# Moving two weight-conversion steps on VectorE, and renumbering PSUM banks, in a fused attention and feed-forward kernel

## The chip, the core and the metric

The kernel runs on one core of a Trainium2 chip. The metric is device time in microseconds (us) of one execution. TensorE is called PE here, with PEld for its weight loads; VectorE is DVE, ScalarE is ACT, GpSimd is POOL, and SP is the engine whose queue issues most DMAs.

## What is computed

Routing attention over 4 batches, 8 heads, 768 positions and 64 dimensions, followed by a feed-forward layer of width 2048 on the 3072 tokens:

```python
q_assign = np.argmax(np.einsum('bhsd,hcd->bhsc', q_n, c_n), axis=-1)   # 16 clusters a head
k_assign = np.argmax(np.einsum('bhsd,hcd->bhsc', k_n, c_n), axis=-1)
mask = q_assign[:, :, :, None] == k_assign[:, :, None, :]
scores = np.where(mask, scale * np.matmul(q, k.transpose(0, 1, 3, 2)), -1e9)
attn = softmax(scores)                       # less the row maximum, over sum + 1e-9
x = matmul(attn, v)                          # laid out as (B*S, H*D) = (3072, 512)
h = x @ w_in                                 # (3072, 2048)
g = h * erf(softplus(h))
out = g @ w_out                              # (3072, 512)
```

## The kernel before

**Two stages.** Attention comes first. It works on 16 pairs: one batch and two heads each, the two heads one below the other on the 128 partitions. Behind it comes the feed-forward layer in 6 chunks of 512 tokens, computed with fast matrix multiplication schemes, so that many sums of blocks stand beside fewer products. In attention, and in most of the feed-forward part, every engine's instructions run in the order in which the code issues them (`InOrder`, whose inner call is the line L132 that nearly all instructions of the profile carry). Each engine is therefore a queue: an instruction that waits holds all behind it on the same engine.

**A pair's six sixths.** `period(p, i)` (L1361) issues sixth i of pair p. A sixth handles two units; a unit u is 128 keys against 384 queries (one half of the queries), for both heads. Sixths 0 to 2 are the first half of the queries, 3 to 5 the second. In a sixth PE's order is, with the helper of each step:

- at sixths 0 and 3 `turn`, which brings row shifts into place;
- `step_ahead` (L1347), a step of `maxima_step` (L460) for later units: four bf16 matmuls into the one tile `wide`, then DVE's reduction `nmx<-wide` over it, the row maxima. A second such step follows in the same sixth, and its first matmuls need the first reduction to be over, for there is only one `wide`;
- `products` (L513): scores into the tile `sc`, two buffers in turn; `scores` (L526) adds the mask;
- at sixth 3 `similarities` (L391) for the pair after next, into the bank `turned[1]`;
- `curve`: ACT's exponentials from `sc` into `pr`;
- `attend`: matmuls of the sixth before, with `v`, into `turned[0]` (first half) or `turned[1]` (second half);
- at the ends of sixths 0 and 3 the first part of `divide` (L574) for the half just finished: matmuls `turned<-more_out,minus`, which sum over the keys what POOL has added up, into the *other* `turned` bank. At sixth 3 that is `turned[1]`, which held the similarities. ACT then takes logarithm and exponential of it, and DVE the quotient (`den`, two `turned<-turned,inv`, and `more_out<-den,turned`) in the sixth that follows.

On POOL `accumulate` (L549) adds the `pr` tiles of a half, unit by unit: five additions a half, each on the result of the one before. `divide`'s matmuls need the last of them.

**The choice of clusters.** `choose` (L404) is a generator that `period` moves on a step at a time through `routing[0]`. Its steps on DVE: a transposition `sims<-turned` of the similarities, a maximum over 16 clusters (`sc<-sims`, into a score bank), the comparison `hot<-sims,sc`, and two more transpositions in sixths 5 and 0. Sixth 3 issues the first three.

**The weights' conversion.** While attention runs, the feed-forward weights are fetched in steps n (256 KB of 64-bit words each) and converted for 22 of 32 steps, two steps a pair, in pairs 1 to 11: n1 = 2p − 1 and n2 = 2p (`early` tells whether a step exists). A step passes through

- `size` and `rest` on ACT (L305, L308), writing into the weight tile `w` and into the fetched place;
- `bounded` (L316) on DVE: a maximum with 2.0 on `w`, 128x512 fp32;
- `sign` (L320) on ACT, which reads and writes the fetched place, not `w`;
- `shifted` (L327) on DVE: a shift left by 3 on `w` as uint32, after `bounded`;
- `summed` (L331) on POOL: adds the fetched place to `w`, after `shifted`, and then issues the fetch of a later step (five further on) into the same place, on SP.

Step n1 has its `bounded`, `sign` and `shifted` in sixth 3 and its `summed` in sixth 4, ahead of that sixth's additions of `accumulate`. The other step, n2, has `bounded` and `shifted` in sixth 0 of the next pair and `summed` in sixth 1.

**Banks in the feed-forward part.** `whole_bank` (L699) counts `n_banks` up and takes entry `n_banks % 8` of a list: entries 0 to 5 are fresh tiles of a pool with six buffers (`bank` in the profile), entries 6 and 7 are the fixed tiles `turned[0]` and `turned[1]`. Chunks 2 to 5 run `hidden49` (L1039) and then `project26` (L1234). `hidden49` computes seven outer products `o`; each begins (L1088) by taking four banks X, N, Y and Z in this order. X is written by four products in turn (`m1`, `m6`, `m7`, `m4`), with an eviction after each; N by `m5`, the second product of the first outer one. `project26` takes 26 banks for as many products and evicts each one product later, the last ones after its loop. A chunk takes 28 + 26 = 54 banks, so its start in the list of eight moves on by 6 from chunk to chunk.

Of the kernel before, what the change touches and what calls it, by code (L numbers as in the profile page):

```python
# [140 lines left out]
def kernel(  # L141
# [174 lines left out]
    def bounded(n):  # L316
        w = w_steps[n][0]
        ve.tensor_scalar(out=w, in0=w, scalar1=2.0, scalar2=None, op0=ALU.max)
# [8 lines left out]
    def shifted(n):  # L327
        w = w_steps[n][0].bitcast(U32)
        ve.tensor_scalar(out=w, in0=w, scalar1=3, scalar2=None, op0=ALU.logical_shift_left)
# [61 lines left out]
    def similarities(p):  # L391

        if p >= NPAIR:
            return
        st = pairs[p]
        st["psim"] = turned[1][:, 0:HW]
        for g in range(4):
            te.matmul(
                st["psim"][2 * C * g : 2 * C * (g + 1)], lhsT=ccT[:, p % HP],
                rhs=st["qk"[g // 2] + "T"][:, (g % 2) * HW : (g % 2 + 1) * HW],  # L400
                start=True, stop=True,
            )
# [57 lines left out]
    def maxima_step(p, i, sm=wide, behind=False, cut=HW):  # L460

        st = pairs[p]
        nmx = maxima[p % 2]
        t, half = divmod(i, 2)
        keys = slice(cut, S) if half else slice(0, cut)
        width = keys.stop - keys.start

        def passes(a, b, start, rows):
            for e in range(2):
                r = slice(e * D + rows.start, e * D + rows.stop)  # L470
                te.matmul(
                    sm[:, e, 0:width], lhsT=st[a][r, t * P : (t + 1) * P],
                    rhs=st[b][r, keys], start=start, stop=not start,
                )

        passes("qv", "kv", True, slice(0, D))
        if behind:
            yield
        passes("qm", "km", False, slice(Q, D) if behind else slice(0, D))
        if behind:  # L480
            yield
        ve.tensor_reduce(
            out=nmx[:, :, t, half], in_=sm[:, :, 0:width], axis=AX.X, op=ALU.max, negate=True
        )
        if i in (NJ - 1, 2 * NJ - 1):
            h = i // NJ
            ve.tensor_reduce(
                out=lowest[h][:, :, ::D].rearrange("p t e -> p e t"),
                in_=nmx[:, :, h * HJ : (h + 1) * HJ], axis=AX.X, op=ALU.min,
            )  # L490
            turns.append((p, h))
# [204 lines left out]
    n_banks = [0]  # L696
# [342 lines left out]
    def hidden49(n):  # L1039
# [33 lines left out]
        def second_forms(which):  # L1073
            for get, new in ((all_own, xb_own), (all_more, lambda i: xb[:, i, 4:])):
                b11, b21, b22, b12 = (get(o) for o in (1, 2, 3, 7))
                for out, a, b in {
                    0: [(new(0), b12, b11), (new(1), b22, new(0)), (b12, b22, b12)],
                    1: [(new(1), b21, new(1))],
                }[which]:
                    minus_of(out, a, b, ge)  # L1080
# [7 lines left out]
        def begin(k):  # L1088
            o = OUTER[k]
            state[o] = {nm: whole_bank() for nm in "XNYZ"}  # L1090
            state[o].update({nm.lower(): t.rearrange("p (j t) -> p j t", t=P) for nm, t in state[o].items()})
            state[o]["m5"] = temps[k % 3]
# [107 lines left out]
        def second_gate():  # L1200
# [5 lines left out]
            (5, m5): lambda: gates_of[2:], (5, m2): lambda: first_steps,  # L1206
            (5, m6): second_gate, (6, m1): lambda: later["soft"][1:], (6, m6): lambda: later["erf"],
        }
        for k, o in enumerate(OUTER):
            begin(k)  # L1210
            p = OUTER[k - 1]
            if k == 0:
                steps = [(m1, o), (m5, o), (m2, o), (m6, o)]
            elif k == 1:
                steps = [(m1, o), (m5, o), (m7, p), (m3, p), (m6, o), (m4, p), (m2, o)]
            elif k < 6:
                steps = [(m1, o), (m7, p), (m5, o), (m3, p), (m4, p), (m6, o), (m2, o)]
            else:
                steps = [(m1, o), (m7, p), (m5, o), (m3, p), (m6, o), (m4, p), (m2, o), (m7, o), (m3, o), (m4, o)]
            for i, (f, which) in enumerate(steps):  # L1220
                f(which)
                for work in extra_of.get((k, f), lambda: [])() if which == o else ():
                    work()
                if k in (0, 4) and f == m2:
                    second_forms(k // 4)
# [115 lines left out]
    def run(work):  # L1341
        for _ in work:
            pass
# [3 lines left out]
    def step_ahead(u, behind=False):  # L1347
        p, i = divmod(u + NJ, 2 * NJ)
        cut = NARROW if u >= 2 * NJ and u // 2 % HJ < HJ - 1 else HW
        steps = maxima_step(p, i, behind=behind, cut=cut) if p < NPAIR else iter(())  # L1350
        if not behind:
            run(steps)
        return steps
# [4 lines left out]
    routing = [iter(())]  # L1358
    part = [iter(())]

    def period(p, i):  # L1361
        u = 2 * NJ * p + 2 * i
        n1, n2 = 2 * p - 1, 2 * p
        early = lambda n: 0 <= n < N_EARLY

        def mask(place):
            which = (MASKS if p else FIRST_MASKS).get((i, place))
            if which:
                return masks(p + 1, *which, turned[0 if i in (0, 5) else 1], place > 1)
            return lambda: None  # L1370

        if u > 0:
            for which in turns if i in (0, 3) else ():
                turn(*which)
                turns.remove(which)
            step_ahead(u)
        mask(0)()
        next(part[0], None)
        if i == 5:
            next(routing[0], None)  # L1380
        if i == 0 and p:
            run(routing[0])
        if u == 2:
            next(routing[0])
        products(u)
        products(u + 1)
        mask(1)()
        second = step_ahead(u + 1, True) if u > 0 else iter(())
        next(second, None)
        rows = D if u == 0 or u + NJ >= len(units) else Q  # L1390
        scores(u, rows)
        next(second, None)
        if i:
            next(second, None)
        next(part[0], None)
        scores(u + 1, rows)
        later = mask(2)
        if i == 0:
            next(second, None)
        if i == 3:  # L1400
            similarities(p + 2)
            routing[0] = choose(p + 2, sc_of[u + 1][:, 0], True)
        if i == 0:
            later()
            later = lambda: None
        curve(u)
        later()
        curve(u + 1)
        if u == 0:
            step_ahead(1)  # L1410
            similarities(1)
            routing[0] = choose(1, turned[0])
            next(routing[0])
            next(routing[0])
            vectors(1, "q")
            vectors(1, "k")
        if i == 0 and early(n1 - 1):
            bounded(n1 - 1)
            shifted(n1 - 1)
        elif i == 1 and early(n1):  # L1420
            size_and_rest(n1)
        elif i == 3 and early(n1):
            bounded(n1)
            sign(n1)
        elif i == 5 and early(n2):
            rest(n2)
        for _ in range(min(len(forms), FORMS.get(p, {}).get(i, 0))):
            forms.pop(0)[0]()
        if i == 3:
            for _ in range(3):  # L1430
                next(routing[0], None)
            if early(n1):
                shifted(n1)
        elif i == 1:
            load(p + 1, "v", v, vp)
            if p == 0:
                run(routing[0])
                transposes(2, "q")
        elif i == 2:
            transposes(p + 2, "k")  # L1440
        elif i == 4:
            vectors(p + 2, "k")
            vectors(p + 2, "q")
        elif i == 5:
            transposes(p + 3, "q")
        if u > 0:
            if i == 4 and early(n1):
                summed(n1)
            for w in (u - 2, u - 1):
                accumulate(w)  # L1450
            if i == 1 and early(n1 - 1):
                summed(n1 - 1)
            if i % HJ == 1 and p in POOL_FORMS and forms:
                forms.pop(0)[1]()
            for w in (u - 2, u - 1):
                attend(w)
            if i % HJ == 0:
                part[0] = divide(u - 1)
                next(part[0])
        if i == 0 and early(n1 - 1):  # L1460
            sign(n1 - 1)
        if i == 3 and early(n2):
            size(n2)
# [186 lines left out]
```

## Time and profile before

| | us |
|---|---|
| median of 3 runs (964.34 to 964.9) | 964.86 |
| profiled execution, time | 965.18 |
| profiled execution, span from first to last instruction | 963.5 |
| attention's last `minus` matmuls, from the start of the span | 414.96 |
| from chunk 4's first product (780.83) to chunk 5's (870.19) | 89.36 |

The granted PE clock is 1.00 over the span. A timeline line has the start in us from the beginning of the span, the length in us, the engine, line and operation, what it writes `<-` what it reads, the shape and the count; brackets give idle time of the engine before it and what ended that. Neighbouring instructions of one kind are merged into a line, with their count. A matmul's end is modelled; its start is measured. Several instructions that work on `w` share the form `w_in<-w_in`: of these, fp32 is `bounded` and uint32 is `shifted`.

### The profile page before, as it was taken

Reading aid. Unit: us, or ns where it says so; the run is one execution under the profiler, and the core shown is the slowest. Engines: PE = TensorE matmul, PEld = TensorE weight load, DVE = VectorE, ACT = ScalarE, POOL = GpSimd, SP = SyncE. Lnnn points to the kernel's source line nnn. Section 1 sums busy time; section 2 is a strip of 40 time slices with the busy share of each in tenths; the row PEclk is TensorE's granted clock in tenths of the full one; section 3 lists DMA queues with packets and bytes.
Section 4 is the critical chain, followed back from the end, with each engine's and each line's share of the span. In section 5 each row is a group of like instructions: output and inputs, shape, how many; then the busy total and the mean of one; then the engine's idle time right before and its main releaser. Section 6 shows DMA issues by size and latency. Waiting matters only on the chain.

```text
span 963.5 us, 22508 instructions
## 1 busy us (share of the span) xinstructions
PE 953.1 (99%) x8954; PEld 721.8 (75%) x8954; DVE 765.4 (79%) x1322; ACT 561.2 (58%) x853; POOL 543.6 (56%) x385
## 2 busy tenths in 40 slices
PE   8999999999999999999999999999999999999998
PEld 3555555555555555588888888998999899989987
DVE  8888888888888886878879878488847966795787
ACT  3778888888887666557624442564258226714651
POOL 1678877777777888935789902550353054206500
PEclk9999999999999999999999999999999999999999
DMA  9444444446444311272994349653564438254523
GB/s 220 79 109 111 110 108 107 109 109 176 89 111 107 71 35 35 65 277 66 183 206 192 147 163 236 207 187 116 191 199 130 162 135 262 77 185 152 157 88 110
DMA packets 180920, 134.41 MB, mean 140 GB/s; under 512 B 131888, under 2 KB 141616, under 8 KB 180784
## 3 DMA queue, kind: packets, MB, share of 16 engines
q1 hardware_dynamic: 173600, 123.37, 44.1%
q0 software_dynamic: 4720, 9.18, 5.4%
q8 instruction: 71, 1.16, 0.5%
q10 hardware_dynamic: 2496, 0.43, 0.2%
q14 instruction: 33, 0.27, 0.1%
HBM read 99.39 MB, written 35.39 MB: 140 GB/s over the span
## 4 chain that ended last, share of the span: by engine, by line
PE 94%; DMA 2%; DVE 2%; POOL 1%; issue 1%; ACT 0%; SPq 0%; DVEq 0%; ACTq 0%; POOLq 0%
PE bank L132 41%; PE turned L132 31%; PE sc L132 16%; PE wide L132 6%; POOL more_out L132 1%; DVE nmx L132 1%; DMA more_in<-a_dram 1%; DMA g_more<-in_moe_w_out_dram 0%; DMA in_k<-in_k_dram 0%; DMA in_q<-in_q_dram 0%; SPq L132 0%; DVE kT L132 0%; ACT pr L132 0%; DVE turned L132 0%; DVE sims L132 0%
## 5 line engine op out<-in xcount | busy, mean ns | idle before, releaser
L132 DVE TENSOR_REDUCE nmx<-wide 128x2 f32<-128x512 f32 (+2 forms) x189 | 180.6, 955 | 62.3 <-PE wide L132 59.7
L132 POOL TENSOR_TENSOR more_out<-more_out,pr 128x768 f32<-128x768 f32 x128 | 217.2, 1697 | 17.4 <-ACT pr L132 9.8
L132 ACT ACTIVATE pr<-sc 128x768 f32<-128x768 f32 x192 | 148.6, 810 | 73.1 <-PE wide L132 54.6
L132 PE MATMUL turned<-pr,in_v 128*32 128x193 f32 x3072 | 144.8, 330 | 0.0
L132 PEld LDWEIGHTS turned<-pr,in_v 128*32 128x32 f32 x3072 | 91.5, 109 | 51.5 <-issue 22.0
L132 DVE TENSOR_TENSOR g<-g,bank 128x512 f32<-128x512 f32 (+1 forms) x139 | 77.9, 578 | 50.7 <-PE bank L132 45.8
L132 PE MATMUL bank<-x_own,w_in 128*128 128x128 f32 (+1 forms) x712 | 106.6, 296 | 0.0
L132 POOL TENSOR_TENSOR x_own<-x_own 128x512 f32<-128x512 f32 x16 | 23.0, 1449 | 146.5 <-DVE x_own L132 133.7
L132 PE MATMUL sc<-qT,kT 64*128 64x384 f32 x528 | 98.5, 486 | 0.0
L132 PEld LDWEIGHTS bank<-x_own,w_in 128*128 128x128 f32 x712 | 94.2, 192 | 4.7 <-DVE g L132 0.8
L132 DVE TENSOR_TENSOR g<-g 128x512 f32<-128x512 f32 x114 | 78.9, 692 | 19.8 <-PE bank L132 14.0
L132 POOL TENSOR_TENSOR more_out<-pr,pr 128x768 f32<-128x768 f32 x32 | 58.9, 1840 | 40.4 <-ACT pr L132 40.4
L132 POOL TENSOR_TENSOR g<-g,osb 128x512 f32<-128x512 f32 x40 | 51.9, 1312 | 49.4 <-DVE g L132 35.7
L132 PE MATMUL bank<-w_out,g 128*128 128x256 f32 x336 | 77.0, 379 | 0.0
L132 PEld LDWEIGHTS bank<-w_out,g 128*128 128x128 f32 x336 | 63.7, 190 | 9.0 <-DVE g L132 0.3
L132 PE MATMUL bank<-g_more,g 128*128 128x256 f32 x288 | 68.3, 380 | 0.0
L132 PE MATMUL wide<-kv,qv 64*128 64x256 bf16 (+2 forms) x378 | 64.0, 328 | 1.1 <-ACT km L132 0.6
L132 PE MATMUL wide<-km,qm 64*128 64x256 bf16 (+3 forms) x378 | 62.5, 327 | 0.0
L132 PEld LDWEIGHTS sc<-qT,kT 64*128 64x128 f32 x528 | 47.9, 187 | 19.2 <-ACT inv L132 2.9
L132 DVE TENSOR_TENSOR g<-a_s,g 128x512 f32<-128x512 f32 x64 | 59.7, 969 | 3.1 <-ACT a_s L132 3.1
L132 ACT ACT_TABLE_LOAD x40 | 51.3, 1283 | 18.5 <-DVE g L132 17.8
L132 PEld LDWEIGHTS bank<-g_more,g 128*128 128x128 f32 x288 | 54.5, 190 | 8.1 <-issue 0.8
(214 smaller groups left out, 1961.3 us busy)
## 6 DMA issues: line engine op xcount, KB each, us to landing
g_more<-b_dram SPq DMA_DIRECT2D x48, 512.0 KB, 3.3
w_in<-a_dram SPq DMA_DIRECT2D x64, 256.0 KB, 3.6
more_in<-a_dram SPq DMA_DIRECT2D x48, 256.0 KB, 3.4
x_own<-in_moe_w_in_dram SPq DMA_DIRECT2D x13, 512.0 KB, 4.0
in_v<-in_v_dram SPq DMA_DIRECT2D x32, 192.0 KB, 3.0
x_dram<-more_out SPq DMA_DIRECT2D x128, 48.0 KB, 2.2
x_own<-x_dram SPq DMA_DIRECT2D x6, 1024.0 KB, 5.5
in_k<-in_k_dram SPq DMA_DIRECT2D x59, 96.0 KB, 2.6
```

The lines of the kernel that those rows point to most:

```text
L132: ins = getattr(self.engine, name)(*args, **kw)
```

## The change

It moves two DVE instructions of step n1 and changes the count of banks. `bounded(n1)` goes from ahead of `choose`'s transposition to right behind it, still in sixth 3. `shifted(n1)` goes from the end of sixth 3 into sixth 4, behind that sixth's first `step_ahead` and so behind its first reduction of row maxima. The order on DVE was `bounded`, transposition, maximum, comparison, `shifted`, row maxima; it becomes transposition, `bounded`, maximum, comparison, row maxima, `shifted`. Step n2 is not touched.

In `hidden49` the count skips six entries when the first bank would be entry 6 or 7. That is so in chunk 2 (it started at entry 7, now at 5) and, since all later starts have moved, in chunk 5 (1 before, 5 now). Chunks 3 and 4 start at 3 and 1 instead of 5 and 3.

```diff
@@ hidden49
+        if (n_banks[0] + 1) % 8 in (6, 7):
+            n_banks[0] += 6
         for k, o in enumerate(OUTER):
             begin(k)
@@ period
             step_ahead(u)
+        if i == 4 and early(n1):
+            shifted(n1)
         mask(0)()
@@ period
         elif i == 3 and early(n1):
-            bounded(n1)
             sign(n1)
@@ period
         if i == 3:
-            for _ in range(3):
+            next(routing[0], None)
+            if early(n1):
+                bounded(n1)
+            for _ in range(2):
                 next(routing[0], None)
-            if early(n1):
-                shifted(n1)
         elif i == 1:
```

## The prediction

> **What bounds the kernel now.** I read the page first.
>
> ```profile
> span 963.5 us, 22508 instructions
> ...
> PE 953.1 (99%) x8954; PEld 721.8 (75%) x8954; DVE 765.4 (79%) x1322; ACT 561.2 (58%) x853; POOL 543.6 (56%) x385
> ...
> PE 94%; DMA 2%; DVE 2%; POOL 1%; issue 1%; ACT 0%; SPq 0%; DVEq 0%; ACTq 0%; POOLq 0%
> ```
>
> PE is busy for 99% of the span and holds 94% of the chain that ended last. A wait of another engine counts only where PE's next instruction hangs on it. The profiled execution took 965.18, 1.7 us more than the span; the sum is made against it and carried over to the median of 964.86, 0.3 lower.
>
> Two of the three edits lie in attention, so I cut its time at the matmuls with `minus` (`divide` in the code), which come at the end of sixths 0 and 3 of each pair. View by windows: stretch, its length, PE busy.
>
> ```profile
> 59.57:71.45 11.88, 11.88 (x172) 6.55 (x176) 10.73 (x18) 9.38 (x17) 9.84 (x6) 1.00 0.37 88
> 71.45:84.16 12.71, 12.66 (x188) 6.92 (x181) 9.81 (x17) 10.67 (x18) 9.82 (x6) 1.00 0.57 129
> 317.31:329.78 12.47, 12.47 (x187) 7.02 (x184) 9.41 (x15) 7.74 (x14) 10.09 (x7) 1.00 0.47 90
> 329.78:341.50 11.72, 11.72 (x180) 6.55 (x175) 10.40 (x17) 7.66 (x14) 9.45 (x6) 1.00 0.09 21
> ```
>
> The first two rows are a pair that converts weights, the last two the same halves after the conversion has ended. Half A (from sixth 3's `minus` to sixth 0's) takes 11.88 against 11.72, half B 12.71 against 12.47. The conversion thus costs PE 0.16 and 0.24 us a pair. Where, the timeline of pair 3 tells (start, length, engine):
>
> ```profile
> 106.55 1.23 DVE L132 TENSOR_REDUCE nmx<-wide 128x2 f32<-128x1024 f32 x1 [1.15 <-PE wide L132]
> ...
> 107.69 0.42 DVE L132 TENSOR_SCALAR w_in<-w_in 128x512 f32<-128x512 f32 x1
> ...
> 108.03 0.58 DVE L132 STREAM_TRANSPOSE sims<-turned 128x384 f32<-128x384 f32 x1
> 108.71 0.56 DVE L132 TENSOR_REDUCE sc<-sims 128x24 f32<-128x384 f32 x1
> 108.72 0.19 PEld L132 LDWEIGHTS turned<-more_out,minus 128*32 128x32 f32 x8 [0.40 <-issue]
> ...
> 109.31 0.55 DVE L132 TENSOR_TENSOR hot<-sims,sc 128x384 bf16<-128x384 f32 x1
> ...
> 109.78 0.42 DVE L132 TENSOR_SCALAR w_in<-w_in 128x512 uint32<-128x512 uint32 x1
> ...
> 110.12 0.68 DVE L132 TENSOR_REDUCE nmx<-wide 128x2 f32<-128x512 f32 x1
> 110.33 1.29 POOL L132 TENSOR_TENSOR w_in<-w_in,x_own 128x512 int32<-128x512 int32 x1 [3.28 <-ACT inv L132]
> ...
> 111.58 1.85 POOL L132 TENSOR_TENSOR more_out<-pr,pr 128x768 f32<-128x768 f32 x1
> ...
> 113.51 6.97 POOL L132 TENSOR_TENSOR more_out<-more_out,pr 128x768 f32<-128x768 f32 x4
> ...
> 120.39 0.88 DVE L132 TENSOR_SCALAR w_in<-w_in 128x512 f32<-128x512 f32 x2
> 120.54 0.22 PEld L132 LDWEIGHTS turned<-more_out,minus 128*32 128x32 f32 x8
> 120.62 0.51 PE L132 MATMUL turned<-more_out,minus 128*32 128x192 f32 x8
> ```
>
> Read it twice. First DVE: it runs without a pause from 106.55, with `bounded` (107.69) ahead of the transposition of the similarities (108.03 to 108.61), and PE's weights for `minus`, whose bank that transposition empties, load only at 108.72: this is half B's 0.24. `shifted` (109.78) then holds back the first maxima of sixth 4 (110.12), which is most of half A's 0.16. Both edits aim at these two places.
>
> Then POOL. `summed` (110.33) adds to what `shifted` wrote and starts 0.13 after it ends at 110.20; the name ACT at the row's end is only the last semaphore that the profile saw. Behind it, in POOL's order, stand the five sums of `accumulate`, end to end: 111.58 begins as `summed` ends, and the four of 113.51 end at 120.48. PE's `minus` of sixth 0 multiplies that sum: its weights load at 120.54, 0.06 later, and its matmul starts at 120.62. How early the load stands elsewhere tells how much PE has left:
>
> ```profile
> 341.34 0.29 PEld L132 LDWEIGHTS turned<-more_out,minus 128*32 128x32 f32 x8
> 341.50 0.51 PE L132 MATMUL turned<-more_out,minus 128*32 128x192 f32 x8
> ...
> 396.61 3.77 POOL L132 TENSOR_TENSOR more_out<-more_out,pr 128x768 f32<-128x768 f32 x2 [0.31 <-ACT pr L132]
> ...
> 400.43 0.16 PEld L132 LDWEIGHTS turned<-more_out,minus 128*32 128x32 f32 x8 [0.23 <-POOL more_out L132]
> 400.43 0.53 PE L132 MATMUL turned<-more_out,minus 128*32 128x192 f32 x8
> ```
>
> Without conversion the load runs 0.16 ahead of its matmul (341.34). Where POOL is plainly late (sums to 400.38), load and matmul both start at 400.43. In pair 3 the load is already held and only 0.08 ahead. **So a chain from `shifted` over `summed` and five sums to PE has 0.08 us of slack, no more.**
>
> **The change part by part.** No instruction is added or removed.
>
> *`bounded` behind the transposition, `shifted` behind the maxima.* Put the rows in the new order. Independent DVE instructions start about 0.08 before their forerunner ends (109.78 plus 0.42 is 110.20, the next at 110.12); the maximum over `sims` needs its forerunner's result and starts 0.10 after it (108.61 to 108.71). New: transposition at 107.69, `bounded` 108.19, maximum 108.53 (its input has long landed, which saves about 0.18), `hot` 109.13, first maxima of sixth 4 at 109.60, `shifted` at 110.20, to 110.62. Before, it ended at 110.20. PE's `minus` of sixth 3 comes 0.24 earlier and the first maxima 0.52 earlier, as meant; but `shifted` ends **0.42 later**.
>
> What hangs on that: `summed` starts at 110.75 instead of 110.33, the five sums follow end to end, the last ends at 120.90, the weights load at 120.96, and sixth 0's `minus` runs then instead of at 120.62: **0.34 late**. PE's order is fixed, so all its work behind stands too. A load that was held costs a little more: the next matmuls come 0.02 later. Half B loses its wait on the transposition, but the sums do not hang on PE's earlier arrival: their chain starts at the maxima of 106.55, which themselves lie a fixed piece of half B behind the last `minus`. A pair thus costs 0.34 + 0.02 = 0.36, less some rounding: 0.35. Conversion steps of this kind stand in pairs 1 to 11 (n1 = 1 to 21): 11 times 0.35 is **+3.8**.
>
> Bounds: if the 0.18 is not saved, `shifted` ends 0.60 later, a pair costs 0.54 and the sum is +5.9. If POOL's chain held nobody, the gain would be 0.24 to 0.40 a pair, −2.6 to −4.4. Both ends stay in the range. I take +3.8, since every link of its chain is a row above.
>
> The Trainium skill speaks against the saved 0.18: "VectorE: DVE Perf Modes", section "The DRAIN you can't avoid", says that a flush follows every DVE instruction and that leaving out semaphores saves nothing. By it the order would not matter and the sum would go to +5.9; the rows at 110.12 (starting before its forerunner ends) and 108.71 (after) agree better with its remark that an instruction that isn't held starts earlier, so the trace decides for +3.8.
>
> What else moves: ACT's `sign` reads another tile than `bounded` and starts where it did. The fetch that `summed` issues goes out 0.42 later on SP; its data is wanted five steps, two and a half pairs, later: no cost, and if that cover went, DMA would show ahead of ACT's `size`.
>
> *The banks.* In chunks 2 and 5 the count of banks skips ahead by six, so X of every outer product leaves the two fixed tiles `turned`.
>
> ```profile
> 601.38 1.06 PE L132 MATMUL bank<-x_more,more_in 128*128 128x128 f32 x8
> 601.79 0.41 DVE L132 TENSOR_TENSOR g_more<-g_more,turned 128x256 f32<-128x256 f32 x1
> ...
> 609.92 0.60 ACT L132 ACTIVATE g<-turned 128x512 f32<-128x512 f32 x1
> 610.59 0.97 PEld L132 LDWEIGHTS turned<-x_own,w_in 128*128 128x128 f32 x8 [0.31 <-issue]
> ...
> 636.61 0.97 PEld L132 LDWEIGHTS turned<-x_own,w_in 128*128 128x128 f32 x8 [0.78 <-issue]
> ...
> 814.92 1.95 PE L132 MATMUL bank<-x_own,w_in 128*128 128x128 f32 x16
> 815.78 1.87 DVE L132 TENSOR_TENSOR g<-g,bank 128x512 f32<-128x512 f32 x3
> ...
> 870.39 0.42 DVE L132 TENSOR_TENSOR g_more<-g_more,bank 128x256 f32<-128x256 f32 x1
> 871.08 1.06 PE L132 MATMUL bank<-x_more,more_in 128*128 128x128 f32 x8
> ```
>
> In chunk 2 PE waits twice for an X in `turned`: 0.31 at 610.59 (ACT empties it until 610.52) and 0.78 at 636.61. In chunk 4 X is a pool tile: its first matmul (the second eight of 814.92, at 815.81) starts while DVE still reads the X before (815.78 to 816.46), so the pool gives another buffer. Both waits go: −1.1. But the first N of chunk 2 now falls on `turned[0]`, which holds the last product of chunk 1, and DVE empties that from 601.79 to 602.20; N's first matmul stood at 601.38. With 0.07 from release to load, as at 610.52, and the matmul close behind, it starts at 602.30: +0.9. Chunk 5 meets the same tile, but DVE is through at 870.81 and N stands at 871.08: nothing. Sum −0.2; bounds −1.1 (DVE comes sooner) to +0.9 (the old waits stay).
>
> Together +3.8 − 0.2 = +3.6: 968.8 against the profiled execution, **968.4** against the median.
>
> **The rivals.** *The edits do what they aim at.* If POOL had 0.42 of slack, a pair would gain 0.24 to 0.40: 960 to 962, faster. It decides at the load of 120.54: this needs sums that end 0.42 later without holding it, against 0.08 measured. Chance 0.12.
>
> *Half of each.* `shifted` gets through earlier than I reckon, or the banks give the whole 1.1 and a pair costs under 0.2: 963 to 966.8. Chance 0.10.
>
> *DVE and POOL shut each other out.* In sixth 0 the next step's `bounded` and `shifted` (120.39) now meet POOL's last sum, 0.42 later than before.
>
> ```profile
> 456.64 1.29 POOL L132 TENSOR_TENSOR w_out<-w_out,osb 128x512 int32<-128x512 int32 x1 [4.82 <-DVE w_out L132]
> 456.76 1.45 DVE L132 TENSOR_SCALAR w_out<-w_out 128x512 f32<-128x512 f32 x1
> ...
> 121.46 1.82 POOL L132 TENSOR_TENSOR more_out<-pr,pr 128x768 f32<-128x768 f32 x1 [0.98 <-ACT pr L132]
> 121.50 0.69 DVE L132 TENSOR_REDUCE nmx<-wide 128x2 f32<-128x512 f32 x1 [0.23 <-PE wide L132]
> ...
> 122.58 0.38 PE L132 MATMUL wide<-kv,qv 64*128 64x512 bf16 x2
> ```
>
> Begun beside a POOL sum, this instruction takes 1.45 instead of 0.42 and ends 0.28 after POOL. `bounded` will so end at about 121.18 and `shifted` is due at 121.21; POOL's next sum, now at 121.46, is due at 121.27, because its input lands 0.19 sooner. Should that sum (1.82) begin ahead of `shifted`, DVE is held until 123.37. The next maxima, now at 121.50 and due at 121.86, would start at 123.3, 1.4 late; PE has 0.39 in hand there (maxima to 122.19, its next `wide` at 122.58) and loses 1.0 a pair: 11 more, near 980. I put it at 0.08, the order being 0.06 in favour of `shifted`. The Trainium skill has the shutting out as a rule ("SBUF — State Buffer", section "Who interferes with whom": one port pair that both use, kept for a whole instruction by whoever comes first).
>
> **How the numbers follow.** Forecast (POOL's chain binds) 0.70, in itself 967.6 to 971.7 (+2.7 with the whole bank gain, +6.8 with both upper bounds). What this measurement can tell from no change is about 0.2%, 1.9 us: faster is under 962.9, slower over 966.8. Faster 0.12, same 0.10, slower 0.70 + 0.08 = 0.78. The range leaves out the first and the last rival, 0.20: 963.0 to 971.8.
>
> **What would show it.** Right: sixth 3's `minus` weights load 0.16 ahead again, `summed` 0.4 later, halves A near 12.45 and B near 12.49, PE's wait named POOL before sixth 0's `minus`; in chunk 2 one wait near 602 in place of two. Wrong: halves A at or under 11.88, or DVE's TENSOR_SCALAR longer than 1 us with B above 13.

## The result and the profile after

The changed kernel takes 968.0 us (median of 6 runs, 967.64 to 968.87) against 964.64 before (6 runs beside it): ratio 1.0036, 95% interval 1.0023 to 1.0049, 3.4 us slower. 968.4 was forecast. The page of the changed kernel:

```profile
span 966.1 us, 22505 instructions
...
PE 92%; POOL 3%; DVE 2%; DMA 1%; issue 1%; ACT 1%; SPq 0%; DVEq 0%; ACTq 0%; POOLq 0%
```

POOL had 1% of the chain that ended last and now has 3%. The same four halves as before, by windows (length, PE busy, then PEld, DVE, ACT, POOL):

```profile
59.29:71.68 12.39, 12.04 (x180) 6.57 (x171) 11.25 (x19) 9.88 (x17) 9.83 (x6) 1.00 0.37 85
71.68:84.18 12.50, 12.50 (x180) 7.05 (x184) 9.71 (x17) 10.03 (x17) 10.04 (x6) 1.00 0.59 131
320.50:333.00 12.50, 12.50 (x180) 7.05 (x184) 9.44 (x15) 7.35 (x13) 10.16 (x7) 1.00 0.46 88
333.00:344.72 11.72, 11.72 (x180) 6.54 (x175) 10.40 (x17) 7.66 (x14) 9.45 (x6) 1.00 0.08 20
```

Half B has lost its wait (12.71 to 12.50), half A has gone from 11.88 to 12.39, and PE's busy time in it is 0.35 short of the length, so PE waits there. Of the halves after the conversion the last is what it was, 11.72; the third, 12.50 instead of 12.47, still begins with a `minus` whose weights were held. The view of waits names the wait in half A:

```profile
PEld turned L132 <- POOL more_out L132: 8.0, 12, 0.7
...
PE turned L132 <- POOL more_out L132: 3.6, 11, 0.3
```

PE's row has it eleven times, once for each pair that converts. The twelfth late weight load is one at 403.65, after the conversion, which the kernel before has too (400.43). Pair 3 in the timeline:

```profile
107.10 1.23 DVE L132 TENSOR_REDUCE nmx<-wide 128x2 f32<-128x1024 f32 x1 [1.15 <-PE wide L132]
...
108.24 0.57 DVE L132 STREAM_TRANSPOSE sims<-turned 128x384 f32<-128x384 f32 x1
...
108.73 0.39 DVE L132 TENSOR_SCALAR w_in<-w_in 128x512 f32<-128x512 f32 x1
108.93 0.26 PEld L132 LDWEIGHTS turned<-more_out,minus 128*32 128x32 f32 x8
109.04 0.55 DVE L132 TENSOR_REDUCE sc<-sims 128x24 f32<-128x384 f32 x1
...
109.62 0.55 DVE L132 TENSOR_TENSOR hot<-sims,sc 128x384 bf16<-128x384 f32 x1
...
110.10 0.68 DVE L132 TENSOR_REDUCE nmx<-wide 128x2 f32<-128x512 f32 x1
...
110.70 0.41 DVE L132 TENSOR_SCALAR w_in<-w_in 128x512 uint32<-128x512 uint32 x1
...
111.25 1.30 POOL L132 TENSOR_TENSOR w_in<-w_in,x_own 128x512 int32<-128x512 int32 x1 [3.64 <-ACT w_in L132]
...
112.09 1.22 DVE L132 TENSOR_REDUCE nmx<-wide 128x2 f32<-128x1024 f32 x1
112.50 1.85 POOL L132 TENSOR_TENSOR more_out<-pr,pr 128x768 f32<-128x768 f32 x1
...
113.36 0.34 PE L132 MATMUL wide<-kv,qv 64*128 64x384 bf16 x2
...
114.42 6.97 POOL L132 TENSOR_TENSOR more_out<-more_out,pr 128x768 f32<-128x768 f32 x4
...
120.70 1.44 DVE L132 TENSOR_SCALAR w_in<-w_in 128x512 f32<-128x512 f32 x2
...
121.45 0.16 PEld L132 LDWEIGHTS turned<-more_out,minus 128*32 128x32 f32 x8 [0.71 <-POOL more_out L132]
...
121.77 2.06 POOL L132 TENSOR_TENSOR more_out<-pr,pr 128x768 f32<-128x768 f32 x1 [0.37 <-ACT pr L132]
```

Sixth 3's weights (108.93) wait for nobody any more, and the first maxima of sixth 4 follow `hot` at once. But `shifted` ends at 111.11, `summed` starts 0.14 later, the five additions of `accumulate` (112.50 and 114.42) end at 121.39 and the weights of sixth 0's `minus` load at 121.45, with 0.71 of idle time of the weight loads put down to POOL. Read against the two times from which the chain starts (106.55 before, 107.10 now), `shifted` ends 4.01 instead of 3.65 after it, 0.36 later.

### The profile page after: what moved, and what is told of

Its sections match the earlier page's. It is cut to its first block, busy times and chain, and to the rows that moved or that the text cites. A ratio compares the mean times of both kernels' runs of the same rounds, so it can differ in the third digit from the quotient of the medians.

```text
span 966.1 us, 22505 instructions
## 1 busy us (share of the span) xinstructions
PE 952.9 (99%) x8954; PEld 723.3 (75%) x8954; DVE 769.7 (80%) x1322; ACT 559.9 (58%) x853; POOL 546.0 (57%) x385
## 4 chain that ended last, share of the span: by engine, by line
PE 92%; POOL 3%; DVE 2%; DMA 1%; issue 1%; ACT 1%; SPq 0%; DVEq 0%; ACTq 0%; POOLq 0%
PE bank L132 42%; PE turned L132 28%; PE sc L132 16%; PE wide L132 6%; POOL more_out L132 3%; DVE nmx L132 1%; DMA g_more<-in_moe_w_out_dram 0%; DMA in_k<-in_k_dram 0%; SPq L132 0%; DMA in_q<-in_q_dram 0%; DVE kT L132 0%; DVE osb L132 0%; ACT pr L132 0%; DVE x_more L132 0%; DVE turned L132 0%
## 5 line engine op out<-in xcount | busy, mean ns | idle before, releaser
L132 PE MATMUL bank<-x_own,w_in 128*128 128x128 f32 (+1 forms) x760 | 112.0, 294 | 0.0
L132 PEld LDWEIGHTS bank<-x_own,w_in 128*128 128x128 f32 x760 | 99.7, 192 | 4.9 <-DVE g L132 1.0
L132 POOL TENSOR_TENSOR more_out<-pr,pr 128x768 f32<-128x768 f32 x32 | 60.9, 1905 | 33.6 <-ACT pr L132 33.2
```

Of the source, the lines that this page charges most:

```text
L132: ins = getattr(self.engine, name)(*args, **kw)
```

## The experiments

Two theories stood against each other: that the loss is POOL's chain behind the later `shifted`, and that it lies in the other parts of the change (the moved `bounded`, DVE's order as such, the banks). Each run stands beside runs of the kernel before on the same chip.

**The moved steps alone**: the changed kernel less

```diff
-        if (n_banks[0] + 1) % 8 in (6, 7):
-            n_banks[0] += 6
```

> The two moved conversion steps without the renumbered banks. If POOL's chain behind the later shift costs about 0.29 us in each of 11 pairs, as the changed kernel's trace reads, this kernel is 3.2 us slower than before: about 967.9, half A 12.39 and half B 12.50. If the loss came from the banks instead, it is at 964.6 or under.

Measured: 967.94 against 964.69, ratio 1.0035 (1.0023 to 1.0048), 3.25 slower. All of the loss is in attention.

**The banks alone**: these two lines added to the kernel before.

> The renumbered banks without the moved steps. If the two waits for X in chunk 2 go and one wait for N near 601 comes, it ends 0.1 to 0.2 us earlier than before, 964.4 to 964.6, or 0.6 earlier if the wait for a transfer in chunk 3 is also gone for a reason that lies in the banks. If the banks carry the loss, it is near 968.

Measured: 964.80 against 964.69, ratio 1.0002 (0.9993 to 1.0011): nothing that can be told from no change. The chunks by windows, chunk 2 first; the kernel before, then the banks alone:

```profile
600.49:690.98 90.49, 89.73 (x602) 83.46 (x600) 68.74 (x118) 43.62 (x67) 28.78 (x24) 1.00 0.55 177
690.98:780.83 89.85, 89.42 (x601) 83.43 (x600) 67.56 (x118) 43.83 (x67) 28.90 (x24) 1.00 0.51 164
```

```profile
600.82:691.18 90.36, 89.65 (x602) 83.51 (x601) 68.60 (x118) 43.82 (x67) 28.82 (x24) 1.00 0.55 177
691.18:780.54 89.36, 89.36 (x601) 83.43 (x600) 67.49 (x118) 43.81 (x67) 28.89 (x24) 1.00 0.51 165
...
602.12 0.41 DVE L132 TENSOR_TENSOR g_more<-g_more,turned 128x256 f32<-128x256 f32 x1
...
602.58 0.97 PEld L132 LDWEIGHTS turned<-x_more,more_in 128*128 128x128 f32 x8 [0.90 <-DVE g_more L132]
```

The forecast's wait for N stands in the last row: 0.90 behind the eviction that ends at 602.53. It replaces waits worth about as much. The 0.49 that chunk 3 is shorter is no gain of the banks, as the same two chunks show in a kernel with the old banks (`bounded` alone moved, below):

```profile
598.05:688.25 90.20, 89.58 (x601) 83.45 (x600) 68.75 (x118) 43.72 (x67) 28.75 (x24) 1.00 0.55 178
688.25:777.62 89.37, 89.37 (x601) 83.43 (x600) 67.51 (x118) 43.80 (x67) 28.91 (x24) 1.00 0.51 165
```

Chunk 3 takes 89.37 there, and chunk 2 takes 90.20, less than with the renumbered banks. The other traces agree: with the old banks chunk 2 takes 90.19 (the moved steps alone) and 90.21 (`shifted` alone moved), with the renumbered ones 90.33 to 90.36 in four traces, and chunk 3 is 89.35 to 89.38 in all traces but that of the kernel before.

**`bounded` alone moved**, `shifted` left where it was:

```diff
         elif i == 3 and early(n1):
-            bounded(n1)
             sign(n1)
...
         if i == 3:
-            for _ in range(3):
+            next(routing[0], None)
+            if early(n1):
+                bounded(n1)
+            for _ in range(2):
                 next(routing[0], None)
             if early(n1):
                 shifted(n1)
```

> Only bounded is moved behind the transposition; shifted stays ahead of sixth 4's first maxima. By the chain theory shifted then ends 0.23 earlier against the minus of sixth 0 of before, POOL's sums hold nobody, half A stays at 11.88 and half B falls from 12.71 to 12.47: 0.236 a pair, 2.6 us faster, about 962.0. If moving bounded were what costs, it is slower than before.

Measured: 962.14 against 964.69, ratio 0.9974 (0.9964 to 0.9984), 2.6 **faster**. Halves A and B of pair 3, and the rows that matter:

```profile
108.34:120.23 11.89, 11.89 (x181) 6.53 (x176) 10.75 (x19) 9.38 (x17) 9.84 (x6) 1.00 0.37 88
120.23:132.70 12.47, 12.47 (x188) 7.02 (x185) 9.68 (x17) 10.42 (x18) 9.81 (x6) 1.00 0.60 132
```

```profile
109.38 0.42 DVE L132 TENSOR_SCALAR w_in<-w_in 128x512 uint32<-128x512 uint32 x1
...
113.11 6.97 POOL L132 TENSOR_TENSOR more_out<-more_out,pr 128x768 f32<-128x768 f32 x4
...
120.14 0.22 PEld L132 LDWEIGHTS turned<-more_out,minus 128*32 128x32 f32 x8
120.22 0.51 PE L132 MATMUL turned<-more_out,minus 128*32 128x192 f32 x8
```

Half B gains its 0.24, half A keeps its length, and the load stands 0.08 ahead of its matmul as before: the gain is had and the slack is not spent.

**`shifted` alone moved**, `bounded` ahead of the transposition as before:

```diff
+        if i == 4 and early(n1):
+            shifted(n1)
...
-            if early(n1):
-                shifted(n1)
```

> Only shifted is moved behind sixth 4's first maxima; bounded stays ahead of the transposition. By the chain theory shifted ends 0.60 later (one reduction of maxima), the sums as much, less about 0.1 of slack, plus 0.02: 0.52 to 0.54 a pair, 5.7 to 5.9 us slower, about 970.4, half A 12.40 and half B 12.73. If the earlier maxima were worth what half A's excess over 11.72 suggests, it would be 1.5 us faster.

Measured: 970.45 against 964.69, ratio 1.0060 (1.0048 to 1.0073), 5.8 slower. Halves A and B:

```profile
110.07:122.45 12.38, 12.03 (x173) 6.58 (x173) 11.24 (x18) 9.89 (x17) 9.83 (x6) 1.00 0.36 84
122.45:135.18 12.73, 12.68 (x180) 6.95 (x181) 9.84 (x17) 10.25 (x17) 10.04 (x6) 1.00 0.58 128
```

The two parts of the change pull against each other: −2.6 and +5.8 alone, together +3.25, which is their sum within the noise.

**POOL's end taken away**, two ways. First, `summed` behind POOL's first addition in the changed kernel:

```diff
-            if i == 4 and early(n1):
-                summed(n1)
             for w in (u - 2, u - 1):
                 accumulate(w)
+            if i == 4 and early(n1):
+                summed(n1)
```

> The changed kernel with summed(n1) issued behind the first addition of accumulate in sixth 4 instead of ahead of it, so that POOL's additions no longer wait for shifted. If POOL's order alone were the trouble, the loss turns into the gain of the moved bounded: 962. But POOL's first addition then starts about 0.35 before sixth 3's minus, 0.03 ahead of bounded on DVE. If DVE's fp32 step is held beside a POOL addition, as its 1.45 us beside POOL in the profile of before reads, bounded ends 1.7 late, the comparison hot as much, and PE, whose next scores need hot's bank, waits 1.4 to 1.7 a pair: 980, with half A near 13.5.

Measured: 962.17 against 964.58, ratio 0.9974 (0.9964 to 0.9984), 2.4 faster. The collision that I expected does not hold PE:

```profile
107.96 2.11 POOL L132 TENSOR_TENSOR more_out<-pr,pr 128x768 f32<-128x768 f32 x1 [1.10 <-DMA in_k<-in_k_dram]
107.99 0.38 DVE L132 TENSOR_SCALAR w_in<-w_in 128x512 f32<-128x512 f32 x1
...
109.95 0.42 DVE L132 TENSOR_SCALAR w_in<-w_in 128x512 uint32<-128x512 uint32 x1
...
120.02 0.29 PEld L132 LDWEIGHTS turned<-more_out,minus 128*32 128x32 f32 x8
120.18 0.51 PE L132 MATMUL turned<-more_out,minus 128*32 128x192 f32 x8
```

`bounded` starts 0.03 behind POOL's addition and still runs its 0.38; it is POOL that is held, 2.11 instead of 1.85. DVE's order is that of the changed kernel, `shifted` after the maxima included, and the load of sixth 0's `minus` is now 0.16 ahead. So that order costs nothing by itself. Nor does moving `shifted` gain anything that these runs can tell: the time is that of `bounded` alone moved, 962.14.

Second, one addition left out, the last one of the second half in pairs 1 to 11, so that the sums under the softmax lack its 128 keys:

```diff
-        if j > 0:
+        if j > 0 and not (half == 1 and j == NJ - 1 and 0 < p <= LAST_X):
```

> The changed kernel without the last of accumulate's five additions for the second half of pairs 1 to 11: the sums under the softmax lack the last 128 keys there, all else is as it was. By the chain theory POOL ends 1.7 earlier than PE's minus of sixth 0 needs it, the minus waits for nobody, and half A is back at 11.88 with half B at 12.47: 0.236 a pair under before, 962 less the 0.1 of the banks. If the loss lay in DVE's order itself and not in POOL's end, it stays near 968.

Measured: 962.29 against 964.58, ratio 0.9977 (0.9967 to 0.9986), 2.3 faster. Halves A and B:

```profile
108.29:120.17 11.88, 11.85 (x180) 6.69 (x176) 10.74 (x19) 9.36 (x17) 8.13 (x5) 1.00 0.36 88
120.17:132.64 12.47, 12.47 (x187) 7.03 (x180) 9.68 (x17) 10.42 (x18) 9.82 (x6) 1.00 0.58 131
```

With POOL 1.7 us shorter in half A, all of the loss is gone. The fetch that `summed` issues (512 KB by the page, not the 256 KB named above) goes out 3.51 after sixth 3's `minus` here as in the changed kernel, and 2.90 before the change. It is as late as there and the time is 962, so its lateness is not what costs.

**Other banks.** The kernel before with

```diff
+        while (n_banks[0] + 1) % 8 in (6, 7):
+            n_banks[0] += 1
```

> The kernel before with the count of banks skipping only to entry 0 when a chunk would start at 6 or 7. X is then a pool tile in chunk 2, and N is not the tile that chunk 1's last product still fills. If the wait for N is what ate the gain of the renumbered banks, chunk 2 is 1.2 to 1.3 us shorter than before: 963.4. If the waits for X come back in another form, there is no change.

Measured: 963.95 against 964.58, ratio 0.9995 (0.9986 to 1.0004). The median lies 0.6 lower, which these runs can't tell from no change. The trace is plainer; chunks 2 and 3:

```profile
600.81:690.17 89.36, 89.36 (x601) 83.43 (x600) 68.55 (x118) 43.65 (x67) 28.75 (x24) 1.00 0.54 179
690.17:779.54 89.37, 89.37 (x602) 83.44 (x601) 67.47 (x118) 43.81 (x67) 28.92 (x24) 1.00 0.50 165
```

Chunk 2 has the length of the others: neither X nor N waits.

**The two gains together**: `bounded` alone moved, and the banks from entry 0.

> The moved bounded alone with the count of banks skipping to entry 0. The two gains are in different stretches and should add: 2.6 and 1.3, about 960.8. If chunk 2's waits depend on when attention ends, 961.5 to 962.1.

Measured: 961.22 against 964.58, ratio 0.9965 (0.9953 to 0.9978), 3.4 faster than the kernel before and 6.8 under the changed one. This is the best version found. It falls short of the 960.8 that I expected because the banks give less: in the traces chunk 2 goes from the 90.20 of the old banks to 89.36, 0.8 and not 1.3; 2.6 and 0.8 are the 3.4 measured.

## Why the prediction was right

*What binds.* The chain `shifted`, `summed`, five additions, `minus` was read from the trace of before with 0.08 of slack, and the runs show it from every side: `shifted` later by one reduction costs 5.8 us; `bounded` alone gains; an addition taken from behind `shifted`, or one left out, turns the loss into the same gain (962.17 and 962.29).

*The size.* The term was 0.35 a pair, 3.8 in all; measured are 0.30 a pair in the windows (half A +0.51, half B −0.21) and 3.25 in the run of the moved steps alone. The term that was mis-sized is the saving of DVE's new order. I gave it 0.18; from the second maxima of sixth 3 to `hot` it was 2.76 (106.55 to 109.31) and is 2.52 (107.10 to 109.62), so 0.24 is saved. Of that, 0.18 is what was forecast: the maximum over `sims` started 0.10 after the end of the transposition, and now (109.04) starts 0.08 before the end of `bounded` (109.12). The other 0.06 the forecast had at nothing: the records are shorter by 0.01 to 0.03 each, `bounded` above all (0.39 for 0.42), and why is not shown. `shifted` is thus 0.36 late, not 0.42; less the 0.08 of slack and plus the 0.02 of the held load, 0.30 a pair.

The total is nearer than its parts, which is luck: attention came out at +3.25 for +3.8, the banks at +0.1, which can't be told from nothing, for −0.2, and the two errors partly cancel in +3.4 for +3.6.

*The Trainium skill's rule* on the flush after each DVE instruction ("VectorE: DVE Perf Modes", "The DRAIN you can't avoid"), by which, taken for every instruction, the order would have saved nothing and the sum come to +5.9, does not fit: the moved steps alone cost 3.25, and the maximum of 109.04 starts before `bounded` ends.

*Where the earlier maxima's gain went.* Half A could have been 11.72 with POOL out of the way; it is 11.88 without the last addition and 11.87 with `summed` behind. In the changed kernel the second maxima of sixth 4 end at 113.31 and PE's next `wide` matmul, which needs them over, starts at 113.36, 4.30 behind the `minus` of half A's begin (109.06). In the kernel before it is 4.30 as well:

```profile
109.06 0.51 PE L132 MATMUL turned<-more_out,minus 128*32 128x192 f32 x8
```

```profile
108.75 0.53 PE L132 MATMUL turned<-more_out,minus 128*32 128x192 f32 x8
...
113.05 0.34 PE L132 MATMUL wide<-kv,qv 64*128 64x384 bf16 x2
```

The first fence is the changed kernel, the second the kernel before. Moving `shifted` behind the first maxima only moves it ahead of the second. DVE has the same work up to there, runs it without a pause, and PE starts 0.05 and 0.06 after its end, so that work sets the time. In the half of before without conversion, where DVE has no `shifted` in it, the same stretch is 4.15 (329.78 to 333.93); the difference of 0.15 is, to 0.01, half A's 11.88 against 11.72.

*The banks.* Both ends were right (no wait for X, one of 0.9 for N), the sum of −0.2 was not: one of the two waits for X, the 0.31 at 610.59, shows in that execution alone and in none of the three other kernels with the old banks. ACT, which empties X, had been held by the landing of a store, and that time varies; the kernel before, then `bounded` alone moved:

```profile
608.95 0.59 ACT L132 COPY osb<-bank 128x512 f32<-128x512 f32 x1 [3.20 <-DMA out_dram<-osb]
```

```profile
605.89 0.58 ACT L132 COPY osb<-bank 128x512 f32<-128x512 f32 x1 [2.58 <-DMA out_dram<-osb]
```

With 2.58 PE does not wait there, and chunk 2 takes the 90.20 shown above. Against that the renumbered banks (90.36) are 0.16 longer. A wait of a single execution was taken for one of the kernel; chunk 3's 0.49 is of the same kind, and both lengthen the profiled execution of before (965.18, with a median of 964.64). That is a part of why the spans differ by 2.6 and the medians by 3.4.

*The rivals.* "The edits do what they aim at" has its condition shown for one edit: once POOL's sums are out of the way the change gains, to 962. But that is `bounded` alone; moving `shifted` gains nothing even then. The rival of DVE and POOL shutting each other out began as described: `bounded` and `shifted` of sixth 0 take 1.44 (120.70) instead of 0.88, since `bounded` meets POOL's last addition and takes 0.98 of it. Then `shifted` comes first, as reckoned, and POOL's next addition is held instead, 2.06 for 1.82, where it has time. The Trainium skill ("SBUF — State Buffer", section "Who interferes with whom") has it that whoever issues first keeps the ports for a whole instruction. The traces agree that one of the two is held (2.06 for 1.82 here); that the first to start wins does not follow from the profile's start times, as the rows of 107.96 and 107.99 show.

What stays open: why the store lands now sooner and now later. It was not tried.

## What to carry to other kernels

Before a step is moved back on an engine with time to spare, follow who waits for it through the other engines, and look for a load that already stands closer to its matmul than elsewhere: that difference is the slack of the whole chain. Here the chain through POOL, busy for 56% of the span, had 0.08 us. Two edits that look like one idea can have opposite signs, so each should be measured alone, and a wait that one profile shows should be looked for in a second profile before it is counted.

## What the runs showed of the hardware

A POOL addition whose record starts 0.03 us ahead of DVE's fp32 `tensor_scalar` did not hold it: DVE took 0.38, POOL 2.11 instead of 1.85 (107.96 and 107.99, `summed` behind). The one that started 0.12 behind POOL's addition in the kernel before (456.76, 1.45 long) was held until 0.28 after POOL's end. So was the `bounded` of sixth 0 in the changed kernel, begun 0.99 behind the start of POOL's last addition: it ended at 121.68, 0.29 after POOL. So of two instructions that start as near to each other as 0.03, the recorded start doesn't tell which one is held; only the one pair of rows shows this.
